# Attention scores in quarters of TensorE's array, and a softmax division moved from GpSimd to VectorE

## The chip, the cores and the metric

The kernel runs on one core of one Trainium2 chip. The metric is the device time of one execution in microseconds (us); lower is better. The core has five engines that work side by side: TensorE (PE in the profile, with its weight loads as PEld), VectorE (DVE), ScalarE (ACT), GpSimd (POOL) and SyncE (SP), which here issues nearly all transfers.

## The reference

The kernel computes a pooled attention and feeds its result to a gated two-layer network. There are 8 batches of 8 heads with 576 tokens and a head width of 64. Keys and values are averaged over groups of 8 tokens, so that 72 pooled positions are left per head.

```python
k_p = k.reshape(B, H, Sp, pool, D).mean(axis=3)        # Sp = 72, D = 64
v_p = v.reshape(B, H, Sp, pool, D).mean(axis=3)
scores = scale * np.matmul(q, k_p.transpose(0, 1, 3, 2))
scores = scores - np.max(scores, axis=-1, keepdims=True)
attn = np.exp(scores)
attn = attn / (np.sum(attn, axis=-1, keepdims=True) + 1e-09)
attn_out = np.matmul(attn, v_p)
x = attn_out.transpose(0, 2, 1, 3).reshape(B * S, H * D)   # 4608 x 512
h = x @ w_in                                               # 512 x 2048
out = (h * np.clip(h + 3.0, 0.0, 6.0) / 6.0) @ w_out       # 2048 x 512
```

All inputs and the output are fp32.

## The kernel before, in words

The 4608 tokens are cut into twelve blocks (`BLOCKS`: 512, 256, then ten of 384). The network is most of the work. The first four blocks run it directly (`Step.h` and `Step.out`, the matmuls of lines 841 and 872). The other eight are taken two at a time as "super blocks" that need seven products instead of eight: one stage of first-layer products (line 1127), then a stage of second-layer products (line 1204 or 1279). Operands are split into a high and a low part, so that one product is three matmuls on fp32r data, one record each in the trace. Scores are plain fp32, two records each.

The attention of a block is a list of small steps (`block_steps`). The steps of a later block are spread over the matmuls of an earlier one: the class `Paced` places a share of them at each slot between two products, so TensorE works on the network and on attention in turns. Instructions of attention on VectorE and ScalarE are kept behind the last instruction of the network that was marked on their engine (`mark`, `after_mark`), and the order of the first part of the program is written out by number in `ORDER` and set by `put_in_order`.

A block's tokens are cut into tiles of 128 (two halves of 64). Where a batch ends inside a tile, the tile has two parts of 64 tokens, one of each batch. For every tile:

- `load_q` loads the queries as [128 rows = two heads of 64, 4 pairs of heads, 128 tokens]. For a tile of two batches it makes two such tiles, each with the other half filled with zeros by GpSimd (line 241).
- `scores` is called twice, for 4 heads each (group g = 0, 1). `Scores.product` (line 465) makes for each of 2 pairs of heads one fp32 matmul with 128 rows, 128 tokens as weights and 144 columns streamed from `kbds`, a block-diagonal matrix with the pooled keys of two heads (72 each) and zeros elsewhere. A tile of two batches needs twice as many matmuls, which add up. `top` takes the negated maximum on VectorE (line 469), `exps` makes four exponentials with their sums on ScalarE (line 474), `invert` adds 1e-9 and takes the reciprocal on VectorE (lines 491 and 492), and `divide` multiplies on GpSimd from the third block on, in one product for 64 of the 72 positions of each head (line 503) and one for the other 8 (line 509).
- `transposes` (lines 574 and 576) turns the attention weights with TensorE, two steps to a tile, two or three groups behind the scores, and splits them with ScalarE and VectorE (lines 585 to 600).
- `av` multiplies with the pooled values (line 648), four steps for each part of a block that belongs to one batch, and ScalarE copies the result (line 650).

The outputs of these small matmuls use the PSUM banks named in `att_banks`, in turn: three (a0, a1, o3) in the first stage of a super block, two (a0, a1) in the second.

`plan` hangs the loading and preparing of K and V of a batch on earlier steps: K from `SIDE` = 12 steps before the first scores of that batch up to these scores (`load_k`, `prep_k`), V from the first scores up to the first product with the values (`load_v`, `prep_v`).

Of the kernel before, what the change touches and what calls it, by code (L numbers as in the profile page):

```python
# [8 lines left out]
F32 = mybir.dt.float32  # L9
# [19 lines left out]
SIDE = 12  # L29
# [36 lines left out]
        454-456 422-425 489-491 476-478 444-447 486-488 479-482 457-460 473-475 492-503 483-485 546-547  # L66
        513-515 504-506 540-542 572-573 554-556 507-509 557-559 543-545 548-550 592-593 551-553 510-512
        522-524 519-521 560-565 525-527 516-518 566-568 528-533 586-588 569-571 574-579 589-591 534-536
        594-599 580-582 537-539 583-585
# [4 lines left out]
        101 75 97 110 98 77-78 102 63 100 79 103 83 81 99 82 64 86 104 84 105 119 88 87 92 124 89 94 62 130  # L74
        93 106 95 125 108 107 120 111 115 109 117 121 116 118 131 128 112 126 134 127 129 68 136 132 66-67
        133 113 65 138 114 123 135 137 140 122 144 139 142 141 150 143 145 152 154 151 147 146 153 156
        148-149 155 157-158 160-161 169 165 163 166-168 170 176 171 164 159 172 181 173 162 182 174 183 175
        177 179-180 184 178 185
# [7 lines left out]
        175 183 177 180-181 179 187 186 184 188 185 194-197 189 202-205 198-199 182 200 208-211 190-191 201  # L86
        206 192 207 212-213 193
    """,
    "Pool": """
        0-1 12 2-3 18 4 7-8 10 5 9 6 14 13 16 15 17 11 19-20 24 21 23 22  # L90
# [3 lines left out]
        35 48 46 43 36 47 39 52 59 42 37-38 45 40 50 49 53-55 57-58 60 56  # L94
# [5 lines left out]
def attention_moe_kernel(  # L100
# [133 lines left out]
    def load_q(tile):  # L234

        qtiles[tile] = []
        for i, (b, s0, n, _) in enumerate(tile):
            t = pool.tile([P, NPAIR, P], F32, name="qt", bufs=2) if i == 0 else ring("qt")
            t = t if i == 0 else t[:, : NPAIR * P].rearrange("p (c t) -> p c t", c=NPAIR)
            if n < P:  # L240
                nc.gpsimd.memset(t[:, :, P // 2 :] if i == 0 else t[:, :, : P // 2], 0.0)
# [198 lines left out]

    class Scores:


        def __init__(self, tile, g):
# [7 lines left out]
            else:  # L452
                self.e = pool.tile([P, 4, SP], F32, name="e", bufs=2)
# [40 lines left out]
        def divide(self, engine):  # L494

            e, sm = self.e, self.sm
            if self.a is None:
# [15 lines left out]
                op=ALU.mult,  # L513
            )
            attn[self.tile, self.g] = self.a

    rests = {}

    def scores(j, tile, g):
# [1079 lines left out]
```

## Time and profile before

| what | value |
| --- | --- |
| time, median of 3 runs | 886.65 us (886.44 to 888.14) |
| the profiled execution: its own time | 887.28 us |
| the profiled execution: its span from first to last instruction | 885.5 us |
| granted TensorE clock, mean | 0.998 |
| ScalarE, exponentials of the attention (line 474, 256 of them) | 324 ns each |
| GpSimd, small division (line 509, 60 of them) | 389 ns each |
| transfers | 200.00 MB, mean 226 GB/s |

The profile comes from one execution. Durations of single instructions are its; a matmul's duration includes the pipeline behind its last element, so the distance of two starts says what it costs in a stream. Each fp32 matmul leaves two records, each with its own weight load. A time in front of a row is counted from the start of the span.

### The profile page before, as it was taken

To read this page: it belongs to the slowest core of one execution; us is meant where nothing else is said; L and a number is where in the kernel's file an instruction comes from. 1 tells how busy PE (TensorE), PEld (TensorE's weight loads), DVE (VectorE), ACT (ScalarE), POOL (GpSimd) and SP (SyncE) were. 2 spreads that over 40 slices of the span, in tenths; PEclk is the share of its full clock that TensorE was granted. 3 is DMA by queue.
4 is the path that set the end of the run, shared out by engine and by line. 5 is a ranking of instruction groups with operands and counts; after the bars stand their busy time and mean duration, and the time that the engine had idled before them with its cause. 6 is when DMAs were issued, how large, how long until landed. Compare 5 with 4: busy or idle time off the path is not lost.

```text
span 885.5 us, 15623 instructions
## 1 busy us (share of the span) xinstructions
PE 868.3 (98%) x5360; PEld 812.0 (92%) x5360; DVE 650.5 (73%) x1322; ACT 551.9 (62%) x1515; POOL 81.4 (9%) x168
## 2 busy tenths in 40 slices
PE   7999999999999999999999999999999999999998
PEld 7788888988989999999888999899999999999998
DVE  5887754567877885878888588987588887466664
ACT  6998766655666654887444688655576756354442
POOL 4100002110111100112000101100110200000000
PEclk9999999999999999999999999999999999999999
DMA  9970206995425254996697969877886687877784
GB/s 315 391 280 0 77 20 202 366 318 161 122 80 161 60 156 123 367 308 214 205 284 234 379 217 288 247 258 246 277 302 219 202 270 243 275 256 239 268 268 134
DMA packets 124654, 200.00 MB, mean 226 GB/s; under 512 B 13216, under 2 KB 81056, under 8 KB 124576
## 3 DMA queue, kind: packets, MB, share of 16 engines
q1 hardware_dynamic: 124432, 199.00, 68.7%
q8 instruction: 43, 0.70, 0.3%
q14 instruction: 35, 0.29, 0.1%
q10 hardware_dynamic: 144, 0.00, 0.0%
HBM read 158.08 MB, written 40.89 MB: 225 GB/s over the span
## 4 chain that ended last, share of the span: by engine, by line
PE 80%; DVE 7%; DMA 7%; ACT 3%; SPq 1%; issue 1%; DVEq 0%; ACTq 0%
PE psx L1127 21%; PE psx L1279 20%; PE pso L872 12%; PE psh L841 12%; PE psx L1204 7%; PE psa L648 4%; PE psa L465 3%; DMA wsFalse<-wd 2%; DMA stage<-q_l 2%; ACT e L474 2%; PE psa L574 1%; DMA wd<-wq 1%; DMA qt<-q_l 1%; DMA wsTrue<-wd 1%; DVE vst L385 1%
## 5 line engine op out<-in xcount | busy, mean ns | idle before, releaser
L1127 PE MATMUL psx<-x,wsFalse 128*128 128x384 f32 x768 | 150.8, 339 | 1.2 <-DMA wsFalse<-wd 1.2
L841 PE MATMUL psh<-xhi,w 128*128 128x384 f32 (+2 forms) x520 | 146.2, 340 | 0.1
L1127 PEld LDWEIGHTS psx<-x,wsFalse 128*128 128x128 f32 x768 | 132.7, 188 | 2.3 <-ACT part L1113 1.2
L1113 ACT CAST part<-g 128x768 fp32r<-128x768 f32 x100 | 83.3, 837 | 75.1 <-PE psx L1279 56.0
L872 PE MATMUL pso<-w,ghi 128*128 128x512 f32 x384 | 120.6, 399 | 0.4 <-ACT o L877 0.4
L1115 DVE TENSOR_TENSOR part<-g,part 128x768 fp32r<-128x768 f32 x100 | 95.1, 955 | 35.1 <-ACT part L1113 34.8
L1127 PE MATMUL psx<-x,wsTrue 128*128 128x384 f32 x576 | 116.1, 340 | 0.1
L1279 PE MATMUL psx<-wsFalse,part 128*128 128x256 f32 x864 | 109.6, 283 | 0.8 <-DVE g L1098 0.4
L1279 PEld LDWEIGHTS psx<-wsFalse,part 128*128 128x128 f32 x864 | 106.4, 190 | 1.6 <-ACT kept L1254 1.0
L1127 PEld LDWEIGHTS psx<-x,wsTrue 128*128 128x128 f32 x576 | 99.6, 188 | 0.8 <-DVE g L1092 0.4
L841 PEld LDWEIGHTS psh<-xhi,w 128*128 128x128 f32 x520 | 93.3, 188 | 7.5 <-DVE g L853 0.4
L474 ACT ACTIVATE e<-psa,mx 128x72 f32<-128x72 f32 x256 | 78.7, 324 | 31.4 <-DVE mx L469 29.7
L841 PE MATMUL psh<-xlo,w 128*128 128x384 f32 (+2 forms) x260 | 87.1, 336 | 0.0
L503 POOL TENSOR_TENSOR a<-e,sm 128x256 f32<-128x256 f32 x60 | 40.2, 671 | 504.4 <-DVE sm L492 414.8
L1279 PE MATMUL psx<-wsTrue,part 128*128 128x256 f32 x648 | 82.1, 283 | 0.0
L1279 PEld LDWEIGHTS psx<-wsTrue,part 128*128 128x128 f32 x648 | 79.6, 190 | 0.0
L1090 ACT ACTIVATE r<-g,small 128x384 f32<-128x384 f32 x96 | 58.5, 622 | 33.6 <-DVE g L1098 33.0
L872 PEld LDWEIGHTS pso<-w,ghi 128*128 128x128 f32 x384 | 68.9, 188 | 11.0 <-ACT o L877 0.7
L872 PE MATMUL pso<-w,glo 128*128 128x512 f32 x192 | 74.6, 399 | 0.0
L1098 DVE TENSOR_TENSOR g<-psx,c 128x384 f32<-128x384 f32 x96 | 52.0, 552 | 28.7 <-PE psx L1127 23.1
L1092 DVE SCALAR_TENSOR_TENSOR g<-r,g 128x384 f32<-128x384 f32 x96 | 54.6, 579 | 14.0 <-ACT r L1090 13.5
L1107 ACT COPY c<-psx 128x384 f32<-128x384 f32 x96 | 44.9, 485 | 23.8 <-PE psx L1127 23.7
(139 smaller groups left out, 1453.9 us busy)
## 6 DMA issues: line engine op xcount, KB each, us to landing
wsFalse<-wd SPq DMA_DIRECT2D x64, 512.0 KB, 4.8
wsTrue<-wd SPq DMA_DIRECT2D x48, 512.0 KB, 4.9
wsFalse<-w2d SPq DMA_DIRECT2D x31, 512.0 KB, 5.0
wsFalse<-w2t SPq DMA_DIRECT2D x27, 512.0 KB, 5.3
wsTrue<-w2d SPq DMA_DIRECT2D x21, 512.0 KB, 5.1
wsTrue<-w2t SPq DMA_DIRECT2D x21, 512.0 KB, 5.3
raw<-w_in_l SPq DMA_DIRECT2D x16, 512.0 KB, 8.4
raw<-w_out_l SPq DMA_DIRECT2D x16, 512.0 KB, 8.9
```

The costliest lines, as they stand in the source:

```text
L474: nc.scalar.activation(self.e[:, h], self.ps[:, h], AF.Exp, bias=self.mx[:, h : h + 1], accum_out=self.sm[:, h : h + 1])
L841: nc.tensor.matmul(self.ps, l[f][:, c, :], r[:, c, :], start=c == 0 and i == 0, stop=c == NCC - 1 and i == 2)
L872: nc.tensor.matmul(pos, l, r, start=f == 0 and i == 0, stop=f == NF - 1 and i == 2)
L1090: nc.scalar.activation(r, src, AF.Relu, bias=half_low, scale=GSCALE / (6.0 * WSCALE))
L1092: nc.vector.scalar_tensor_tensor(out=g_of[i][:, k], in0=r, scalar=GSCALE, in1=src, op0=ALU.min, op1=ALU.mult)
L1098: nc.vector.tensor_tensor(out=g_of[i][:, k], in0=ps, in1=kept, op=ALU.add)
L1107: nc.scalar.copy(c, ps)
L1113: nc.scalar.copy(t[:, 0], src)
L1115: nc.vector.tensor_tensor(out=t[:, 1], in0=src, in1=t[:, 0].bitcast(F32), op=ALU.subtract)
L1127: nc.tensor.matmul(ps, w[:, l, c * P : (c + 1) * P], t[:, r, c], start=o in (1, 2, 5) and c == 0 and k == 0, stop=c == 1 and k == 2, skip_ ...
L1204: nc.tensor.matmul(to, l, w[:, qs, r], start=f == 0 and k == 0, stop=end and k == 2)
L1279: nc.tensor.matmul(to, t[:, l, k, i * P : (i + 1) * P], w[:, k, r], start=begin and k == 0 and y == 0 and i % 2 == 0, stop=m == NM - 1 and ...
```

## The change

From the third block on (block index j > 1), `block_steps` uses the new class `TileScores` in place of two calls of `scores` per tile. It does this for all eight heads of a tile:

- `product` makes 16 fp32 matmuls: for each of 4 pairs, for each head r of the pair and for each half x of the tile's tokens, one with 64 rows (head r), 64 columns of weights (the half's queries) and 72 streamed elements (this head's pooled keys, without the zeros). Head r goes to bank r of two banks, half x to partitions 64x to 64x + 63. The four matmuls of a pair thus lie in four different quarters of the array. Outside the written-out part each is kept behind the one before it. The two maxima follow at once, one per bank (288 elements each).
- `exps(0)` and `exps(1)` make the exponentials of four heads each, as steps of their own.
- `finish`, in the same step as `exps(1)`, adds 1e-9 and takes the reciprocal once for eight heads, then makes four products, in place in the tile of the exponentials for the 64 positions. It runs on VectorE, but for the first tile of the third block, which stays on GpSimd.

The transposes of a tile follow a whole tile later; at the end of a block an empty step stands in front of them. `load_q` loads a tile of two batches into one tile without zero fills, and `Scores.product`, still used for the first two blocks, writes the two batches of a tile to their own partitions with 64 columns of weights each. `SIDE` becomes 16, V is prepared from two steps before the first scores on, and the numbers in `ORDER` follow the changed instructions.

```diff
-SIDE = 12
+SIDE = 16
...
+        t = pool.tile([P, NPAIR, P], F32, name="qt", bufs=2)
         for i, (b, s0, n, _) in enumerate(tile):
-            t = pool.tile([P, NPAIR, P], F32, name="qt", bufs=2) if i == 0 else ring("qt")
-            t = t if i == 0 else t[:, : NPAIR * P].rearrange("p (c t) -> p c t", c=NPAIR)
-            if n < P:
-                nc.gpsimd.memset(t[:, :, P // 2 :] if i == 0 else t[:, :, : P // 2], 0.0)
-            nc.sync.dma_start(t[:, :, i * (P // 2) : i * (P // 2) + n], q[b, :, :, s0 : s0 + n])
+            mine = t[:, :, i * (P // 2) : i * (P // 2) + n]
+            nc.sync.dma_start(mine, q[b, :, :, s0 : s0 + n])
             after_mark()
-            qtiles[tile].append(t)
+            qtiles[tile].append(mine)
...
-                for r, (qt, (b, _, _, _)) in enumerate(zip(qtiles[self.tile], self.tile)):
-                    nc.tensor.matmul(to, qt[:, p, :], kbds[b % 2][:, p, :], start=r == 0, stop=r == last)
+                for r, (qt, (b, _, n, _)) in enumerate(zip(qtiles[self.tile], self.tile)):
+                    nc.tensor.matmul(
+                        to[r * (P // 2) : r * (P // 2) + n], qt[:, p, :], kbds[b % 2][:, p, :], start=True, stop=True
+                    )
...
+    class TileScores:
...
+        def product(self):
+            tile = self.tile
+            banks = att_bank(), att_bank()
+            self.mx, self.sm = (pool.tile([P, NG, 4], F32, name=f"{m}s", bufs=2) for m in ("mx", "sm"))
+            halves = [slice(x * D, (x + 1) * D) for x in range(2)]
+            before = last_pe() if len(window) == 2 else None
+            for p in range(NPAIR):
+                for r in (1, 0):
+                    for x, half in enumerate(halves):
+                        part = x % len(tile)
+                        b = tile[part][0]
+                        nc.tensor.matmul(
+                            banks[r][half, p * SP : (p + 1) * SP],
+                            qtiles[tile][part][halves[r], p, half if len(tile) == 1 else slice(0, D)],
+                            kbds[b % 2][halves[r], p, r * SP : (r + 1) * SP],
+                            start=True,
+                            stop=True,
+                        )
+                        if before:
+                            behind(traced[-1], before)
+                        before = traced[-1].name
...
+            for r in (1, 0):
+                to = self.mx.rearrange("p g (i r) -> p (g i) r", r=2)[:, :, r]
+                nc.vector.tensor_reduce(out=to, in_=self.ps[r], axis=AX.X, op=ALU.max, negate=True)
+                self.later()
...
+        def finish(self, engine):
+            e, sm = self.e, self.sm
+            nc.vector.tensor_scalar(out=sm, in0=sm, scalar1=1e-9, scalar2=None, op0=ALU.add)
+            nc.vector.reciprocal(sm, sm)
+            rest = rests[self.tile] = pool.tile([P, NG, 2 * REM], F32, name="ar", bufs=2)
+            for g in range(NG):
+                to = e[:, g].rearrange("p h s -> p (h s)")[:, : 4 * D]
+                engine.tensor_tensor(
+                    out=rest[:, g].rearrange("p (c h s) -> p c h s", c=2, h=4),
+                    in0=e[:, g, None, :, D:].broadcast_to([P, 2, 4, SR]),
+                    in1=sm[:, g, None, :, None].broadcast_to([P, 2, 4, SR]),
+                    op=ALU.mult,
+                )
+                engine.tensor_tensor(
+                    out=to.rearrange("p (h s) -> p h s", h=4),
+                    in0=e[:, g, :, :D],
+                    in1=sm[:, g, :, None].broadcast_to([P, 4, D]),
+                    op=ALU.mult,
+                )
+                attn[self.tile, g] = to
...
-        for t in tiles_of[j]:
+        for n, t in enumerate(tiles_of[j] if j > 1 else ()):
+            x, by = TileScores(t), nc.vector if n or j > 2 else nc.gpsimd
+            steps.append((loads_behind(t), x.product, "scores", [b for b, *_ in t]))
+            steps.append(([], lambda x=x: x.exps(0), None, ()))
+            steps.append(([], lambda x=x, by=by: (x.exps(1), x.finish(by)), None, ()))
+            while todo:
+                turn()
+            todo.extend((t, g) for g in range(NG))
+        if j > 1:
+            steps.append(([], None, None, ()))
+
+        for t in tiles_of[j] if j < 2 else ():
...
-                side_steps(b), ("scores", "av"), (begin - SIDE, begin), (begin, uses("av", b)[0])
+                side_steps(b), ("scores", "av"), (begin - SIDE, begin), (begin - 2, uses("av", b)[0])
```

More of the change, by code (lines that the diff above doesn't have):

```diff
@@ L85 @@
         154 151 149 155 157 160 156 152 166 158 161 159 167 170-172 162-163 168 164 173 165 174 176 178 169
[L86 to L87 removed]
+        175 183 177 180-181 179 187 186 184 188 185 189 198-201 194-195 182 196 204-207 190-191 197 202 192
+        203 208-209 193
     """,
     "Pool": """
[L90 removed]
+        0-1 12 2-4 7-8 10 5 9 6 14 13 16 15 11 17-20
     """,
@@ L439, in pool_second @@
         place_rest(1, rest[:, :, :D])
+    exps_of = {}
     class Scores:
@@ L452, in __init__ @@
             else:
-                self.e = pool.tile([P, 4, SP], F32, name="e", bufs=2)
+                if g == 0:
+                    exps_of[tile] = pool.tile([P, NG, 4, SP], F32, name="e", bufs=2)
+                self.e = exps_of[tile][:, g]
                 self.a = None
@@ L459, in product @@
             ps = att_bank()
-            last = len(self.tile) - 1
             for i in range(2):
@@ L497, in divide @@
             if self.a is None:
-                self.a = pool.tile([P, 4 * D], F32, name="a", bufs=3)
                 if self.g == 0:
@@ L501, in divide @@
                 self.rest = rests[self.tile][:, self.g]
+                self.a = e.rearrange("p h s -> p (h s)")
             copies = 3 if self.first else 2
[L503 to L514 removed]
@@ L515, in divide @@
-            attn[self.tile, self.g] = self.a
+            main = self.a[:, : 4 * D].rearrange("p (h s) -> p h s", h=4), e[:, :, :D], sm[:, :, None].broadcast_to([P, 4, D])
+            rest = (
+                self.rest.rearrange("p (c h s) -> p c h s", c=copies, h=4),
+                e[:, None, :, D:].broadcast_to([P, copies, 4, SR]),
+                sm[:, None, :, None].broadcast_to([P, copies, 4, SR]),
+            )
+            for to, x, y in (main, rest) if self.first else (rest, main):
+                engine.tensor_tensor(out=to, in0=x, in1=y, op=ALU.mult)
@@ new lines, in divide, with last_pe, __init__, exps @@
+            attn[self.tile, self.g] = self.a
+    def last_pe():
+        return next(i for i in reversed(traced) if i.engine == mybir.EngineType.PE).name
+    class TileScores:
+        def __init__(self, tile):
+            self.tile = tile
+        def product(self):
[19 more added lines that the diff above has]
+                        before = traced[-1].name
+            self.ps = [x[:, : NPAIR * SP].rearrange("p (n s) -> p n s", s=SP) for x in banks]
+            self.e = pool.tile([P, NG, 4, SP], F32, name="e", bufs=2)
+            self.later = after_mark if late else no_slot
+            for r in (1, 0):
+                to = self.mx.rearrange("p g (i r) -> p (g i) r", r=2)[:, :, r]
+                nc.vector.tensor_reduce(out=to, in_=self.ps[r], axis=AX.X, op=ALU.max, negate=True)
+                self.later()
+        def exps(self, g):
+            for h in range(4):
+                nc.scalar.activation(
+                    self.e[:, g, h],
+                    self.ps[h % 2][:, 2 * g + h // 2],
+                    AF.Exp,
+                    bias=self.mx[:, g, h : h + 1],
+                    accum_out=self.sm[:, g, h : h + 1],
+                )
+                self.later()
+        def finish(self, engine):
[16 more added lines that the diff above has]
+                    op=ALU.mult,
+                )
+                attn[self.tile, g] = to
```

25 lines of the change are left out of this document (7 added, 18 removed).

## The prediction

> **What bounds the kernel now.** I read the page's busy lines first, then the chain that ended last, then the costliest groups kept apart by shape, and then TensorE's waits.
>
> ```profile
> PE 868.3 (98%) x5360; PEld 812.0 (92%) x5360; DVE 650.5 (73%) x1322; ACT 551.9 (62%) x1515; POOL 81.4 (9%) x168
> ...
> PE 80%; DVE 7%; DMA 7%; ACT 3%; SPq 1%; issue 1%; DVEq 0%; ACTq 0%
> ```
>
> TensorE is busy 98% of the span and holds 80% of the chain. What shortens its work shortens the kernel almost one for one; what lengthens VectorE, at 73%, costs nothing on average and can still cost in a crowded stage. So the first question is what the scores cost TensorE. First two places where they stand in the stream (start, duration, engine, line, operation, count), then their group and those of the softmax (count, busy time, mean ns of one, idle before):
>
> ```profile
> 38.50 1.14 PE L465 MATMUL psa<-kbd,qt 128*128 128x144 f32 x8
> ...
> 188.60 0.65 PE L465 MATMUL psa<-kbd,qt 128*128 128x144 f32 x4
> ```
>
> ```profile
> L465 PE MATMUL psa<-kbd,qt 128*128 128x144 f32 x288 | 45.8, 287 | 0.5 <-DVE arem L600 0.3
> ...
> L503 POOL TENSOR_TENSOR a<-e,sm 128x256 f32<-128x256 f32 x60 | 40.2, 671 | 504.4 <-DVE sm L492 414.8 <-ACT r L1090 24.2 <-ACT wq L945 17.3
> ...
> L469 DVE TENSOR_REDUCE mx<-psa 128x4 f32<-128x288 f32 x72 | 31.8, 450 | 15.5 <-PE psa L465 15.4
> ...
> L491 DVE TENSOR_SCALAR sm<-sm 128x4 f32<-128x4 f32 x72 | 14.0, 198 | 23.7 <-ACT e L474 19.6 <-POOL a L503 2.5 <-ACT stage L474 1.0
> ...
> L492 DVE RECIPROCAL sm<-sm 128x4 f32<-128x4 f32 x72 | 12.6, 176 | 1.7 <-DVE sm L491 0.2
> ...
> L241 POOL MEMSET qt<- 128x256 f32 x8 | 2.5, 315 | 39.8 <-DVE ksum L265 27.2 <-PE psa L465 11.2 <-DVE vlo L398 1.4
> ...
> L503 DVE TENSOR_TENSOR a<-e,sm 128x256 f32<-128x256 f32 x4 | 1.7, 420 | 0.0
> ...
> L509 DVE TENSOR_TENSOR ar<-e,sm 128x64 f32<-128x64 f32 x4 | 0.8, 216 | 0.0
> ```
>
> The 287 ns of one score record is mostly pipeline: four take 0.65 us, so they start (0.65 - 0.287) / 3 = 0.121 us apart, and eight take 1.14 us, which gives (1.14 - 0.287) / 7 = 0.122 us. That pitch, not 287 ns, is what a record costs TensorE. One fp32 matmul leaves two records here (a tile of one batch has 2 groups of 2 matmuls and the trace has 4 records in a group), so such a tile costs 8 x 0.122 = 0.98 us and a tile of two batches, with twice the matmuls, 1.95 us. From the third block on there are 30 tiles; batches change inside a tile at tokens 1728, 2880 and 4032, so 27 are of the first kind and 3 of the second: 26.4 + 5.9 = 32.2 us, 3.6% of the span. That is all that the change can work on in TensorE.
>
> **Part by part.** The sum is made against the profiled execution: span 885.5 us, its own time 887.3 us, which is 0.6 us above the median of 886.65 us.
>
> *Scores in quarters.* A tile now has 4 pairs x 2 heads x 2 halves of its tokens = 16 matmuls, each 64 rows by 64 columns of the array with 72 elements streamed, so 32 records. A record of 144 elements has a pitch of 0.122 us, one of 72 then 0.061 us if the stream sets it. The trace has no matmul in a quarter of the array, so I bound it. If four run at once, a tile costs 32 x 0.061 / 4 = 0.49 us; if two, 0.98 us; if none, 1.95 us. Against 32.2 us, 30 tiles then cost 14.6 (-17.6), 29.3 (-2.9) or 58.6 us (+26.3). One row speaks on the weight loads, which go from 8 to 32 a tile and from 128 columns to 64:
>
> ```profile
> 76.35 0.30 PEld L648 LDWEIGHTS psa<-a,vrem 96*128 96x128 f32 x2
> 76.41 0.39 PE L648 MATMUL psa<-a,vrem 96*128 96x64 f32 x2
> ```
>
> ```profile
> L648 PEld LDWEIGHTS psa<-a,vrem 96*128 96x128 f32 x8 | 1.2, 191 | 0.0
> ```
>
> Here fp32 matmuls stream only 64 elements (0.054 us by the pitch above), yet two weight loads of 128 columns take 0.30 us with 0.191 us for one, so they start 0.11 us apart: with a short stream the weight load sets the pitch. For 64 columns that is about 0.055 us, below the 0.061 us of the stream, so the loads alone don't push a quarter's pitch up. They do if all 32 go through one door (32 x 0.055 = 1.76 us). I take the middle between two and four at once, 0.046 us a matmul or 0.73 us a tile: consecutive matmuls name four different quarters and two banks, so there is always another quarter to start, but the two records of one matmul share a quarter and follow each other. 30 x 0.73 = 22.0 us, a gain of 10.2 us.
>
> *Changing the array's shape.* Each tile goes from the whole array to quarters and back, 60 changes that the trace never shows. The nearest row is a matmul that restarts an idle array:
>
> ```profile
> 197.19 0.44 PE L841 MATMUL psh<-xhi,w 128*128 128x384 f32 x1
> ```
>
> ```profile
> L841 PE MATMUL psh<-xhi,w 128*128 128x384 f32 x256 | 72.8, 341 | 0.1
> ```
>
> It takes 0.44 us instead of 0.341 us: 0.10 us for a first weight load of 128 columns with nothing to hide behind. For 64 columns that is 0.05 us, 3.0 us for 60 changes. The lower end is zero. The upper end is the whole tail of a record (0.287 - 0.122 = 0.165 us) with the 0.10 us load behind it, 0.27 us a change, 16 us. I stay near the lower end because only the first load of a run is exposed in the row. The Trainium skill, "TensorEngine Tiling (Array Packing)", Key Properties, speaks against the change here: it says that a change of tiling mode, unlike a change of tile, drains TensorE. By that the tail is paid at every change, and the sum would be some 10 to 13 us worse; no run here shows it yet.
>
> *The division on VectorE.* Per tile it gets two main products and two small ones, 2 x (420 + 216) = 1.27 us, on 29 tiles (the first tile of the third block stays on GpSimd): 36.9 us. It loses one add and one reciprocal per tile (198 + 176 ns), since both now serve eight heads: 30 x 0.374 = 11.2 us. Net +25.7 us on VectorE, to 676 us or 76%. The two maxima per tile stay (288 elements each). Behind these instructions on VectorE's queue stand the gate and split operations that TensorE needs next, so the cover is VectorE's slack, and it is thinnest here (columns: stretch, length, then busy time of PE, PEld, DVE, ACT, POOL, then clock, DMA share, GB/s):
>
> ```profile
> 380.00:420.00 40.00, 39.67 (x240) 38.56 (x239) 32.98 (x81) 29.88 (x107) 7.52 (x13) 1.00 0.80 248
> 500.00:540.00 40.00, 40.00 (x244) 39.79 (x243) 32.37 (x69) 29.89 (x92) 5.38 (x11) 1.00 0.80 266
> 540.00:580.00 40.00, 38.19 (x253) 37.51 (x252) 34.49 (x76) 29.01 (x91) 5.42 (x12) 0.96 0.85 272
> 660.00:700.00 40.00, 40.00 (x263) 39.87 (x261) 33.24 (x77) 29.61 (x98) 4.22 (x8) 1.00 0.68 213
> ```
>
> The 12 GpSimd instructions of the third stretch are about three tiles; three tiles' net of 0.90 us bring VectorE from 34.5 to 37.2 of 40 us. That still fits.
>
> *GpSimd's wait goes.* TensorE's waits (us in total, times, longest) name the division on GpSimd, and one place and the stretch behind it show what it did:
>
> ```profile
> PE psa L574 <- POOL a L503: 2.1, 2, 1.4
> ...
> PE psa L648 <- DVE a L565: 0.9, 2, 0.5
> ```
>
> ```profile
> 565.99 0.44 PE L574 MATMUL psa<-ident,a 128*128 128x128 f32 x2 [1.38 <-POOL a L503]
> ```
>
> ```profile
> 567.20:570.80 3.60, 3.60 (x18) 3.60 (x19) 3.48 (x9) 3.02 (x7) 0.00 (x0) 0.53 0.93 307
> ```
>
> The transpose of the weights of attention waited 1.38 us, and right behind it the granted clock was 0.53 for 3.6 us, worth another 1.7 us: 3.8 us with the other wait. A later transpose (a tile behind instead of two groups behind) takes the place of these waits, but the reciprocal and the V loads ahead of it can be late too, so I count half, -2 us.
>
> *Longer bursts.* A tile's chain grows: two maxima instead of one, eight exponentials in a row, one late division for all heads, and two banks held from the first product to the last exponential. In the last stage of a super block there are only two banks for all of attention. The chain shows what four exponentials take (8 records with their sums):
>
> ```profile
> 191.63 1.22 ACT e L474 x8
> ```
>
> If whatever follows in the two banks waits for the second four, that is 1.2 us; at most once in each of ten blocks, 12 us; zero if the pacing spreads it. I count +2 us, since the steps of a tile lie apart in time by more than that. Only the last tile of a block has little time to its transposes (two steps); the others have a whole tile's steps.
>
> *Edits with one answer.* Eight zero fills of q tiles on GpSimd go (0.315 us each, on an engine that is 9% busy). The same q loads are issued, into one tile instead of two. Loading and preparing K up to 16 steps ahead instead of 12, and V from two steps earlier, follow the greater number of steps in a block, so in time they move little; SP's queue keeps its number of transfers. The hand-written order of the start moves a few instructions. The one two-batch tile of the second block now uses 64-column matmuls too: 16 records, at most 0.98 us gained, left out of the sum.
>
> Sum: -10.2 + 3.0 - 2 + 2 = -7.2 us, 880.1 us in the profiled execution's terms, **879.5 us** against the median.
>
> **Rivals.**
>
> *Four at once.* All quarters run together; a tile costs 0.49 us, 7.3 us below the forecast: 872 us. For it: four neighbours in the stream never share a quarter. Against: both records of a matmul do.
>
> *Two at once.* Starts stay in the order of issue, so a matmul's second record waits 0.061 us for its first, and the next quarter waits behind it: 16 x 0.061 = 0.98 us, what a tile costs today. Gain 2.9 instead of 10.2 us: 887 us, no difference. The Trainium skill, "TensorE: Matmul & The Clock Gate", Part 3, The mechanism, has a rule that leads here: packed matmuls start and end strictly in program order, though neighbours in different tiles may start some nanoseconds apart. No run here shows it yet, since the trace of before has no packed matmul.
>
> *VectorE becomes the bound.* Where it is already over 80% busy (380-420, 500-580 and 660-700 us; their 44 GpSimd instructions are some 11 tiles) the 0.90 us that each tile adds delays the gate or the split of the next product and TensorE waits as long: 11 x 0.90 = 10 us, 890 us, slower. It decides once TensorE's idle time in these stretches grows by over 7 us. For it: 34.5 of 40 us. Against: the largest wait of TensorE on VectorE in the list above is 0.9 us in all.
>
> *No overlap.* The quarters run one after another, so the change doesn't do what it says: +26.3 instead of -10.2 us, 916 us, slower. For it: the 0.11 us pitch of weight loads shows that they can set the pace. Against: nothing but the quarters' independence.
>
> **How the numbers follow.** Forecast 0.48, four at once 0.16, two at once 0.12, VectorE 0.12, no overlap 0.12. Measurements of this kernel can tell 0.2%, 1.8 us, from no change. The first two are faster and hold 0.64; of "two at once" most is within 0.2% and the rest goes each way; of VectorE's case a little falls back within or below it: faster 0.66, same 0.10, slower 0.24. The range goes from 868 us (four at once with GpSimd's waits fully gone) to 893 us (VectorE's case with its drains); outside it stay "no overlap" and a few hundredths at the ends. The forecast's own range is 875 to 884 us.
>
> **What would show it.** Right: 32 score records a tile within about 0.75 us from first to last start, TensorE's score work down by 10 us, the next record after each run late by about 0.05 us, VectorE near 676 us, no TensorE wait on GpSimd. Wrong: a score run of 1 us or more, a restart of 0.2 us at each change of shape, TensorE waits on VectorE or on exponentials (banks) of several us in the stretches above, or a low clock somewhere new.

## The result and the profile after

The changed kernel takes 896.0 us (median of 4 runs, 894.66 to 896.6) against 886.55 us before (886.44 to 888.14): a ratio of 1.0101 with a 95% interval of 1.0085 to 1.0117, so 9.5 us or 1% slower (the 886.65 us given above was the median of the three runs there were then). The profiled execution spans 894.5 us. The page has these two lines (busy time of each engine, and the chain that ended last):

```profile
PE 867.8 (97%) x6056; PEld 798.2 (89%) x6056; DVE 658.1 (74%) x1378; ACT 550.6 (62%) x1515; POOL 19.7 (2%) x44
...
PE 71%; DVE 12%; DMA 8%; ACT 4%; SPq 2%; issue 2%; DVEq 0%; ACTq 0%
```

TensorE's share of the chain falls from 80 to 71%, and VectorE's rises from 7 to 12%. VectorE's busy time rises by only 7.6 us. The scores themselves do what they should. Three rows of the timeline, around one tile, and the group of all of them:

```profile
192.23 0.34 PE L919 MATMUL psh<-xhi,w 128*128 128x384 f32 x1
192.50 0.73 PE L534 MATMUL psa<-kbd,qt 64*64 64x72 f32 x32
193.16 0.44 PE L919 MATMUL psh<-xhi,w 128*128 128x384 f32 x1
193.43 0.34 PE L919 MATMUL psh<-xlo,w 128*128 128x384 f32 x1
```

```profile
L534 PE MATMUL psa<-kbd,qt 64*64 64x72 f32 x960 | 22.8, 230 | 0.8 <-ACT e L554 0.8
```

A record takes 230 ns, and 32 of them end 0.73 us after the first began: their starts span 0.50 us, 16 ns apart on average, where 0.061 us would be one after the other. The single records of the trace show how: they start in fours, 6 to 7 ns apart within a four and 62 to 63 ns from one four to the next (113 ns to the second). All four quarters run at once, each at the 0.061 us that the prediction gave to one record. The first record starts 0.27 us after a network matmul instead of the usual 0.17 (0.10 us late); behind the last start pass 0.16 us to the next record, and that one costs another 0.10 us. The tile as a whole costs 1.20 - 2 x 0.173 = 0.85 us instead of 0.98; over all 30 tiles I read 0.86 us, so TensorE's score work is 32.2 - 25.8 = 6.4 us shorter.

The loss lies elsewhere. I set the start of every network matmul of the two traces against its namesake: the difference is +1.3 us at 348 us, +9.0 at 358 us and +8.6 at the end. (It goes up and down by a few us in between, since scores now stand at other places.) That is the start of the first super block. The longest of TensorE's waits after, then VectorE's and TensorE's timeline there, and stretches with their granted clock (length, busy time of PE, PEld, DVE, ACT, POOL, then clock, DMA share, GB/s):

```profile
PE psx L1205 <- DVE g L1176: 4.1, 1, 4.1
```

```profile
353.24 0.69 DVE L1024 TENSOR_TENSOR wq<-wq 128x512 fp32r<-128x512 f32 x1 [0.73 <-ACT wq L1023]
358.50 0.56 DVE L1176 TENSOR_TENSOR g<-psx,c 128x384 f32<-128x384 f32 x1 [4.56 <-DMA wd<-wq]
```

```profile
349.43 0.40 PE L950 MATMUL pso<-w,glo 128*128 128x512 f32 x1
...
353.64 1.34 PE L1205 MATMUL psx<-x,wsFalse 128*128 128x384 f32 x6 [0.53 <-ACT c L1185]
359.11 3.25 PE L1205 MATMUL psx<-x,wsFalse 128*128 128x384 f32 x9 [4.13 <-DVE g L1176]
```

```profile
355.00:356.00 1.00, 0.00 (x0) 0.00 (x0) 0.00 (x0) 0.56 (x2) 0.00 (x0) 1.00 0.92 336
356.00:359.00 3.00, 0.00 (x0) 0.00 (x0) 0.50 (x1) 0.00 (x0) 0.00 (x0) 0.51 0.98 269
359.00:363.00 4.00, 3.89 (x12) 3.75 (x13) 2.59 (x10) 2.80 (x11) 0.00 (x0) 0.51 0.98 352
```

What are `wq` and `wd`? The super blocks multiply with sums of first-layer weights. VectorE and ScalarE make them beside the third and fourth block, in 16 links (`sums_of`). Each link fills the tile `wq`; four transfers store it to DRAM (`wd`), from where the super blocks load it as `ws`. There is one `wq`, so a link's first instruction waits for the stores of the link before. The first gate product `g` of the super block lies in memory that `wq` had. So after the last link ended at 353.9 us (353.24 + 0.69), its stores had to land, the gate product began at 358.5, and TensorE stood 4.1 us. Its granted clock was half for 6.8 us, from 356.1 to 362.9 us. TensorE stood idle for the first 3.0 us of that, so the slow clock met 3.8 us of work and cost 1.9 us. (The expectations below count the whole 6.8 us, 3.4 us lost; that is too much.) In the kernel before, the last link ended at 347.6 us, 0.5 us ahead of the last matmul of the plain blocks at 348.1:

```profile
346.93 0.69 DVE L946 TENSOR_TENSOR wq<-wq 128x512 fp32r<-128x512 f32 x1 [0.73 <-ACT wq L945]
...
348.11 0.40 PE L872 MATMUL pso<-w,glo 128*128 128x512 f32 x1
```

Of the 7.7 us between the two places (+1.3 and +9.0), 4.7 are waits (4.13 and 0.53), 1.9 the clock; most of the rest is that two whole tiles of scores stand in this stretch, where the kernel before has half a tile.

Why was it late? VectorE's waits between 300 and 350 us, first before, then after:

```profile
DVE g L853 <- ACT g L849: 5.4, 6, 1.8
...
DVE wq L939 <- DMA wd<-wq: 0.6, 1, 0.6
```

```profile
DVE wq L1017 <- DMA wd<-wq: 7.7, 4, 3.6
...
DVE g L931 <- ACT g L927: 1.4, 3, 0.7
```

Before, VectorE had other work while the stores of a link were under way, and in this stretch lost 0.6 us to them. After, the link's first instruction (line 1017) comes to the head of VectorE's queue too early and holds up everything behind it for 7.7 us in all. (Over all 16 links it is 12.5 us before and 19.6 after.) The links have run out of room: the last ones follow each other at the pace of compute, store and wait.

TensorE's second-longest wait is new too (0.1 us before). It is for the gate of the plain blocks:

```profile
PE psh L919 <- DVE g L931: 3.4, 5, 1.0
```

The longest of these five, at 267 us, stands behind a link that had itself waited 4.1 us for stores; what made the other four is not shown.

### The profile page after: what moved, and what is told of

Its sections match the earlier page's. It is cut to its first block, busy times and chain, and to the rows that moved or that the text cites. A ratio compares the mean times of both kernels' runs of the same rounds, so it can differ in the third digit from the quotient of the medians.

```text
span 894.5 us, 16699 instructions
## 1 busy us (share of the span) xinstructions
PE 867.8 (97%) x6056; PEld 798.2 (89%) x6056; DVE 658.1 (74%) x1378; ACT 550.6 (62%) x1515; POOL 19.7 (2%) x44
## 4 chain that ended last, share of the span: by engine, by line
PE 71%; DVE 12%; DMA 8%; ACT 4%; SPq 2%; issue 2%; DVEq 0%; ACTq 0%
PE psx L1205 22%; PE psx L1357 19%; PE psh L919 9%; PE pso L950 8%; PE psx L1282 7%; PE psa L715 3%; DMA wd<-wq 3%; ACT e L554 1%; PE psa L534 1%; SPq L1026 1%; DMA raw<-w_in_l 1%; PE psa L641 1%; DVE g L1170 1%; DMA wsFalse<-wd 1%; DMA raw<-w_out_l 1%
## 5 line engine op out<-in xcount | busy, mean ns | idle before, releaser
L1205 PE MATMUL psx<-x,wsTrue 128*128 128x384 f32 x576 | 113.8, 339 | 0.1
L919 PEld LDWEIGHTS psh<-xhi,w 128*128 128x128 f32 x520 | 93.1, 188 | 12.7 <-DVE g L931 4.7
L950 PEld LDWEIGHTS pso<-w,ghi 128*128 128x128 f32 x384 | 69.0, 188 | 12.5 <-ACT o L955 0.8
L554 ACT ACTIVATE e<-psa,mxs 128x72 f32<-128x72 f32 x240 | 73.2, 329 | 11.1 <-DVE mxs L549 10.9
L1176 DVE TENSOR_TENSOR g<-psx,c 128x384 f32<-128x384 f32 x96 | 52.2, 551 | 28.8 <-PE psx L1205 17.9
L950 PE MATMUL pso<-w,glo 128*128 128x512 f32 x192 | 72.8, 396 | 0.0
L1170 DVE SCALAR_TENSOR_TENSOR g<-r,g 128x384 f32<-128x384 f32 x96 | 52.2, 552 | 13.7 <-ACT r L1168 13.4
L935 ACT CAST ghi<-g 128x384 fp32r<-128x384 f32 (+2 forms) x65 | 33.1, 509 | 32.5 <-DVE g L931 30.9
```

Of the source, the lines that this page charges most:

```text
L554: nc.scalar.activation(self.e[:, g, h], self.ps[h % 2][:, 2 * g + h // 2], AF.Exp, bias=self.mx[:, g, h : h + 1], accum_out=self.sm[:, g, ...
L919: nc.tensor.matmul(self.ps, l[f][:, c, :], r[:, c, :], start=c == 0 and i == 0, stop=c == NCC - 1 and i == 2)
L950: nc.tensor.matmul(pos, l, r, start=f == 0 and i == 0, stop=f == NF - 1 and i == 2)
L1170: nc.vector.scalar_tensor_tensor(out=g_of[i][:, k], in0=r, scalar=GSCALE, in1=src, op0=ALU.min, op1=ALU.mult)
L1176: nc.vector.tensor_tensor(out=g_of[i][:, k], in0=ps, in1=kept, op=ALU.add)
L1205: nc.tensor.matmul(ps, w[:, l, c * P : (c + 1) * P], t[:, r, c], start=o in (1, 2, 5) and c == 0 and k == 0, stop=c == 1 and k == 2, skip_ ...
```

## The experiments

Each run has a ratio to runs of the kernel before on the same chip (medians 886.3 to 887.8 us in the five groups).

### First group: is it the late chain or VectorE's load?

Theory A: one chain is late at one place. Theory B: VectorE's greater load. Differences to the changed kernel are taken from its 896.0 us, which come from another set of runs; taken from the ratios they differ by up to 1.6 us.

`e1_share45`, attention of the sixth block asked for earlier:

```diff
-        (3, att_steps(5), (), 0.6),
+        (3, att_steps(5), (), 0.45),
```

> The changed kernel with one number edited: the attention of the sixth block is spread over 0.45 instead of 0.6 of the slots of the fourth block, so it ends earlier. Theory A (one late chain): the changed kernel loses its time in one place, where the first super block starts. The sixth block's attention ends later, the operands made from it come later on VectorE, the last weight sums behind them end at 354 instead of 348 us, and the first gate product waits for them (4.1 us) and pays a halved clock after that (about 3.4 us). Then this kernel takes some 7 us less than the changed one, about 889 us, its last weight sum ends before 349 us and the 4 us wait is gone. Theory B (VectorE's load): the divisions on VectorE delay gates and splits all over the kernel; then this stays within 2 us of 896 us.

Measured 896.76 us, ratio 1.010 (1.0079 to 1.0122). The edit missed its aim: the scores stayed at the same places in TensorE's order (all runs of score records but two, which moved by a few matmuls), which behind the numbered part is made when the program is built, from modelled times. The last link ended at 354.6 us. It tells nothing between A and B.

`e2_pool_div`, all divisions on GpSimd as before:

```diff
-            x, by = TileScores(t), nc.vector if n or j > 2 else nc.gpsimd
+            x, by = TileScores(t), nc.gpsimd
```

> The changed kernel with all divisions of the new class on GpSimd, as before the change. Theory B (VectorE's load): the 36 us of divisions are the loss, so this takes 888 us or less. Theory A (one late chain): the late chain stays, 894 to 898 us, with the wait of about 4 us at the start of the first super block still there.

Measured 893.18 us, 1.0051 (1.0034 to 1.0067): 2.8 us better. That is just below what A said (894 to 898) and far above what B said (888 or less); the wait at the first super block is still there (3.5 us in two). But the last link now ended at 347.8 us, as early as before, and 6.3 us were still lost at that place. So the link's clock time alone isn't it; more on this below.

`e3_before_vec_div`, the kernel before with the divisions on VectorE:

```diff
-        s.divide(nc.vector if j == 1 else nc.gpsimd)
+        s.divide(nc.vector if j == 1 or len(window) == 2 else nc.gpsimd)
```

> The kernel before with only the engine of the division changed: VectorE instead of GpSimd, from the first tile behind the written-out part on. Theory B (VectorE's load): slower by 5 to 10 us, 892 to 897 us. Theory A (one late chain): within 2 us of 886.6 us, since the steps and their places stay as they were.

Measured 890.75 us, 1.0028 (1.0015 to 1.0041). Between the theories: the division alone costs some 3 us. The table below puts 2.4 us of them at the same place.

`e4_full`, the changed kernel with scores by the whole array, four heads to a bank, for 29 of the 30 tiles:

```diff
+                        nc.tensor.matmul(
+                            banks[p // 2][part * D : part * D + n, p % 2 * 2 * SP : (p % 2 + 1) * 2 * SP],
+                            qtiles[tile][part][:, p, :],
+                            kbds[b % 2][:, p, :],
```

> The changed kernel with the scores made by the whole array again (four matmuls of 144 elements a tile, eight for a tile of two batches, one bank for four heads); grouping by tile, division, pacing stay as changed. The rows of the two traces say that a tile of one batch costs TensorE 0.98 us on the whole array and 0.86 us in quarters with the change of shape included, so theory A and theory B both expect 3 to 7 us more than the changed kernel, 899 to 903 us; if the quarters were no gain, 896 us or less.

Measured 888.85 us, 1.0013 (0.9996 to 1.003). Both theories missed (899 to 903). Taking the quarters away gains 7 us, though they make TensorE's work shorter. The last link ended at 346.7 us and no long wait followed there.

### Second group: the quarters, or the order that is made of them?

I wrote one kernel's order of instructions on every engine, behind the written-out part, into the other (a list of numbers, set with `behind` as `put_in_order` does).

```python
for x, y in zip(numbers, numbers[1:]):
    behind(by[mine[y]], end.get(mine[x], mine[x]))
```

`e6_full_in_quarter_order`, whole-array scores in the changed kernel's order:

> The mirror image: whole-array scores, in the order of the changed kernel. Theory C: 896 plus 6 us of score work = 902, 898 to 905, and the wait on the gate product near 350 us is back. Theory D: 887 to 890, without that wait.

Measured 898.28 us, 1.0129 (1.0105 to 1.0153). The long wait is back, and of the 30 tiles only the first still uses quarters:

```profile
PE psx L1410 <- DVE g L1381: 4.1, 1, 4.1
```

So the wait comes with the order, not with what the quarters do on the chip. With the same work as `e4_full` it is 9 us slower. Against the changed kernel, which has the same order, it also gives the price of the quarters themselves: they are 2.3 us faster than the whole array, though TensorE's score work is 6.4 us less.

`e5_quarters_in_full_order`, the mirror image:

> The changed kernel, with the instructions of TensorE, VectorE, ScalarE, GpSimd and the DMA queue from the third block on put into the order that the kernel with whole-array scores (888.85 us) has; a tile's 32 records stand where the last of its whole-array matmuls stood. Theory C (the quarters cost nothing on the chip beyond their own 0.86 us a tile; what was lost comes from the order that the scheduler makes of them): 888.9 less some 6 us of score work = 883, 880 to 886, with no wait of several us on the gate product near 350 us. Theory D (the quarters themselves cost the rest of the engines or the clock something, in any order): 892 to 898.

Measured 903.71 us, 1.0185 (1.0163 to 1.0206). A clear miss. TensorE now waited for exponentials:

```profile
PE psa L831 <- ACT e L742: 13.3, 8, 3.1
```

The records stood where the second half of the whole-array matmuls had been, so the first half's exponentials came too late for the transposes. `e16_quarters_at_first` (run later) put them where the first half had been:

> Quarters in the order of the kernel with whole-array scores, as in the run of that name, but with a tile's records and maxima where the first of its whole-array matmuls and maxima stood, so that the exponentials start no later than there. Order is the loss: 888.9 - 6 = 883, 880 to 886, and the waits on exponentials are gone. The quarters cost something on the chip in any order: 892 to 898.

Measured 904.26 us, 1.0188 (1.0164 to 1.0212), and another wait had taken the place:

```profile
PE psa L718 <- ACT e L742: 8.1, 5, 3.3
```

L718 is the score product itself. Eight heads at once need two free banks at once, and one of them is still being read by the exponentials of the tile before; two groups of four need one bank at a time. So the order of one doesn't fit the other at either end, and these two runs don't give the price of the quarters. Both lie above either forecast (880 to 886, or 892 to 898).

`e7_side12`, the plan of K and V loads as before:

```diff
-SIDE = 16
+SIDE = 12
...
-                side_steps(b), ("scores", "av"), (begin - SIDE, begin), (begin - 2, uses("av", b)[0])
+                side_steps(b), ("scores", "av"), (begin - SIDE, begin), (begin, uses("av", b)[0])
```

> The changed kernel with the side steps of a block planned as before (12 steps ahead instead of 16, the second half 2 steps later). If the plan's shift makes the late chain: 887 to 890. If the place that the scheduler gives the quarters does: 894 to 898.

Measured 890.67 us, 1.0026 (1.0009 to 1.0044): 5.3 us of the 9.5 go with the two numbers of the plan. The last link ended at 349.7 us, and no halved clock followed.

`e8_quarter_after_quarter`, a tile's products sorted by quarter:

```diff
-            for p in range(NPAIR):
-                for r in (1, 0):
-                    for x, half in enumerate(halves):
+            for r in (1, 0):
+                for x, half in enumerate(halves):
+                    for p in range(NPAIR):
```

> The kernel of the first of these runs with a tile's 16 products sorted by quarter, so that eight records in a row use the same quarter, where neighbours used different ones. If quarters run beside each other only when neighbours differ: a whole-array record of 144 columns takes 0.122 us, so one of 72 some 0.061; 32 of them 1.96 us instead of 0.51 us, 29 tiles: 42 us above the first run. If order inside a tile does not matter: within 2 us of the first run.

Measured 919.09 us, 1.0363 (1.0335 to 1.039), 15.4 us above `e5_quarters_in_full_order` ("the first run"), between the two forecasts. The run of a tile:

```profile
194.20 1.63 PE L718 MATMUL psa<-kbd,qt 64*64 64x72 f32 x32
```

Starts are (1.63 - 0.23) / 31 = 0.045 us apart on average instead of 0.016: most follow at 56 to 63 ns, and only some start with a neighbour, 5 to 6 ns behind it. So neighbours in different quarters are what makes them overlap. 29 tiles x 0.9 us are 26 us; some 4 us of that took the place of waits for exponentials (13.3 us in `e5`, 9.0 here), and where the rest went I didn't settle.

### Third group: move the wait

`e9_gate_elsewhere`: the gate tiles of the first super block are allotted in reverse order, so that the first doesn't lie on `wq`. TensorE's order is unchanged.

```diff
+        if n == 0:
+            for i in reversed(range(0, NPR, 2)):
+                pairs[i // 2] = late[1].tile([P, 2, 4, HALF], F32, name=f"g{i}")
```

> The changed kernel with one edit: the gate's result tiles of the first super block are allotted in the reverse order, so that the first gate product writes memory that the weight sums' tile wq did not lie in. TensorE's order stays what it was. If the loss is the late weight-sum chain that the first gate product waits for: the 4.1 us wait and the halved clock of 6.8 us behind it (3.4 us) go, 896 - 7.5 = 888.5, 887 to 890. If something else on the way is late as well and takes the wait's place: 893 to 896.

Measured 895.94 us, 1.009 (1.0076 to 1.0104): nothing gained. The gate's wait is gone and this one has come:

```profile
PE psx L1208 <- DMA wsTrue<-wd: 4.7, 1, 4.7
```

The super block also loads the sums that the last link stores. The second reader of the chain was late by as much as the first. With the same edit, `e10_gate_pool` (divisions on GpSimd), `e11_gate_side12` (plan as before) and `e12_gate_side12_pool` (both):

> The same edit on the changed kernel with all divisions on GpSimd (893.18 us with its wait of 3.5 us and 3.4 us for the halved clock). Late chain: 893.2 - 6.9 = 886.3, 885 to 889. VectorE's load as a second term of its own: 2 to 4 us below the run with the divisions on VectorE and the tiles elsewhere; if the divisions only acted through the late chain: within 1 us of it.

> The same edit on the changed kernel with the plan of the side steps as before (890.67 us, waits on the gate product of 2.5 us in all and no halved clock). Late chain: 890.7 - 2 = 888.7, 888 to 890.5. If the plan costs by itself, beside the chain: 2 us or more below the run with the new plan and the tiles elsewhere.

> Quarters alone: plan as before, divisions on GpSimd as before, and the gate's tiles elsewhere. The score work of TensorE is 6.5 us less than before. If nothing else is lost: 887.4 - 6.5 = 881, 880 to 884. If the divisions cost nothing and a loss of 8 us that is neither chain nor division remains: within 1.5 us of the run with the plan as before, near 889.

Measured 895.05 us (1.0075, 1.0058 to 1.0091), 891.16 us (1.0038, 1.0024 to 1.0052) and 892.19 us (1.0046, 1.0032 to 1.0059). In each the wait for `ws` stands in the gate's place (4.0, 2.2 and 2.5 us), so the gains that a vanished chain was to bring (885 to 889, 888 to 890.5 and 880 to 884 us) did not come; for the third neither forecast held. The plan is worth 4.8 us here with the divisions on VectorE and 2.9 with them on GpSimd; the divisions 0.9 us, or nothing.

### Fourth group: shorten the chain itself

`e13_one_sum_less` and, as control, `e14_before_one_sum_less` leave out one of the 16 sums and store the sum before it a second time in its place, so their output is not the reference's:

```diff
+        if (i, h) == (NPR - 1, 0):
+            t = last_sums[0]
+            for o, at in {7: 0, 3: 1, 5: 2, 6: 3}.items():
+                nc.sync.dma_start(dram_of(i, o)[:, :, half], t[:, :, at])
+            return
```

> The changed kernel without the work of one of the 16 weight sums, the last but one: its stores are made from the sum before it, so that the transfers stay and one link of the chain (some 8 us) is gone; the output is not the reference's. If the late end of the weight sums is the loss: the wait at the first super block goes, 896 - 7.5 = 888.5, 887 to 890. If it is only a place where time shows that was lost earlier: 893 to 896.

> Control: the kernel before with the same link left out. Its last weight sum ends before the plain blocks do, so nothing should wait for it: 887.4 within 1.5. If the 4 us of VectorE work that is left out pays by itself: 883 to 885.

Measured 889.08 us (1.002, 1.0007 to 1.0034), 7 us better than the changed kernel, and 885.84 us (0.998, 0.9964 to 0.9997), 1.8 us better than before, between the control's two forecasts. So up to 1.8 of the 7 us may come from the work left out, and at least 5 from the chain. In the first, the last link ends ahead of its block, and VectorE's gate product waits for its operand alone:

```profile
348.18 0.69 DVE L1032 TENSOR_TENSOR wq<-wq 128x512 fp32r<-128x512 f32 x1 [0.69 <-ACT wq L1031]
...
353.97 0.56 DVE L1184 TENSOR_TENSOR g<-psx,c 128x384 f32<-128x384 f32 x1 [1.69 <-PE psx L1213]
```

`e15_two_sums_tiles` keeps all sums but breaks the chain: high parts and sums get tiles of their own, two for the sums, each link makes eight stores instead of four, and the links of the fourth block are asked for earlier. To make room, the ring of small tiles has 3 instead of 4 (`e17` and `e18` below too).

```diff
-        return pool.tile([P, S], F32, name=name, tag="ring", bufs=4)
+        return pool.tile([P, S], F32, name=name, tag="ring", bufs=3)
...
-        t = early_x[-1].tile([P, 2, 4, P], F32, name="wq", bufs=1)
-        hi, q = t[:, 0], t[:, 1]
+        hi = early_x[-1].tile([P, 4, P], F32, name="wh", bufs=1)
+        q = early_x[-1].tile([P, 4, P], F32, name="wq", bufs=2)
...
-        hooks[2 + n // NPR].setdefault(2 * (n % NPR), []).append(step)
+        hooks[2 + n // NPR].setdefault(2 * (n % NPR) if n < NPR else 3 * (n - NPR) // 2, []).append(step)
```

> The changed kernel with all weight sums, but with a tile of their own for the high parts and two for the sums, so that a sum need not wait for the stores of the one before, and asked for earlier in the last plain block; the ring of small tiles has 3 instead of 4 to make room. If the late end of the weight sums is the loss: 887 to 891. If not, or if the doubled number of stores or the shorter ring cost as much: 893 to 898.

Measured 889.18 us, 1.002 (1.0006 to 1.0035), 6.8 us better, with no sum left out. TensorE's order is another one here too, so the run by itself doesn't tell the two tiles from the earlier links. The last link ends 17 us ahead:

```profile
327.44 0.69 DVE L1024 TENSOR_TENSOR wq<-wq,wh 128x512 fp32r<-128x512 f32 x1 [2.46 <-ACT wh L1023]
```

For every kernel, how late the last link ends against the start of the last matmul of the plain blocks, and how long from there to the 61st first-layer record of the super block, both read from the traces in us:

| kernel | late | then |
| --- | --- | --- |
| before | -0.5 | 10.2 |
| before, one sum less | -5.7 | 9.9 |
| quarters, two sums tiles (`e15`) | -17.0 | 10.4 |
| the same, plan as before (`e18`) | -15.8 | 10.8 |
| the same, plan and divisions as before (`e17`) | -12.8 | 10.8 |
| quarters, one sum less | -1.5 | 10.7 |
| whole array (`e4_full`) | 0.1 | 10.9 |
| before, division on VectorE | 1.6 | 12.7 |
| quarters, plan as before | 2.0 | 13.6 |
| quarters, division on GpSimd | 2.2 | 16.5 |
| quarters in the whole array's order (`e16`, `e8`, `e5`) | 1.0, 1.4, 1.6 | 14.4, 13.3, 12.8 |
| gate elsewhere, plan or divisions or both as before (`e12`, `e11`, `e10`) | 1.5, 1.7, 2.0 | 14.0, 15.2, 16.4 |
| attention of the sixth block earlier (`e1`) | 4.0 | 19.2 |
| **the changed kernel** | 4.5 | 17.9 |
| quarters, gate elsewhere | 4.5 | 18.1 |
| whole array in that order | 4.6 | 18.2 |

Where the link ends no later than 0.1 us, the stretch takes 9.9 to 10.9 us; at 1.0 to 2.2 us late 12.7 to 16.5; at 4 us and more 17.9 to 19.2. This also settles the second run: there the plain blocks ended 3.8 us earlier than in the changed kernel and the link 6.1 us earlier, which left it 2.2 us late. It matters which comes last, and not when.

### Fifth group: what is left

`e17_two_sums_side12_pool` (two sums tiles, plan and divisions as before, so of the change only the quarters and the grouping by tile) and `e18_two_sums_side12` (the same with the divisions on VectorE):

> Quarters with the weight sums in two tiles, the plan of the side steps as before and the divisions on GpSimd as before. If the plan and the divisions take the gain away: 882 to 886, below both kernels. If TensorE's saved 6.5 us is lost to waits for other engines whichever they are: 887 to 891.

> The same with the divisions on VectorE. If the divisions cost by themselves: 2 to 4 us above the run with GpSimd's; if only the plan matters: the same as it and below the run with the new plan (889.2), near 885; if neither: 888 to 891.

Measured 883.7 us (0.9963, 0.9951 to 0.9975) and 885.18 us (0.9983, 0.9972 to 0.9994). The first beats both kernels: 2.6 us below before and 12 below the changed kernel. Its busy line and chain:

```profile
PE 863.4 (98%) x6056; PEld 797.0 (90%) x6056; DVE 639.9 (73%) x1262; ACT 549.7 (62%) x1515; POOL 80.6 (9%) x160
...
PE 77%; DVE 8%; ACT 5%; DMA 5%; SPq 3%; issue 1%; DVEq 0%; ACTq 0%
```

With the late chain out of the way, the plan costs 889.2 - 885.2 = 4.0 us and the divisions 1.5 us. The two profiled executions put most of the plan's 4.0 us at another single place: at 427 us, in the first super block, `e15` waits for a copy on ScalarE and runs at half the granted clock from 428.9 to 432.3 us, and `e18` does neither.

```profile
PE psa L715 <- ACT x L717: 1.9, 1, 1.9
```

Two tiles for the sums weren't run on the kernel before; one sum less was worth 0.2% there, so about half of the 0.37% may belong to the chain and not to the quarters.

## Why the prediction was wrong

The forecast was 879.5 us and faster; the kernel is 1% slower, outside the range of 868 to 893 us.

*Scores in quarters* (-10.2) and *changing the array's shape* (+3.0): the net of -7.2 us stood against -6.4 us measured, but both terms were mis-sized, and that their sum came out near is luck. A tile's records span 0.50 us and not 0.73, as in the rival "four at once". Going in and coming out cost 0.10 and 0.26 us, 0.36 us a tile, where I had 0.10. Not all of it is the change of shape: behind four whole-array score records of the kernel before, too, the next record costs 0.10 us more, but it starts 0.03 us behind the last start instead of 0.16. The rule in the Trainium skill, "TensorEngine Tiling (Array Packing)", Key Properties, that a change of mode drains TensorE points the way of these rows, but they don't show a whole drain: 0.16 us is less than the 0.23 us that the last record takes. The rival "two at once" falls: four records start within 20 ns, so the second record of a matmul didn't hold up the next quarter by 0.061 us. On this, "TensorE: Matmul & The Clock Gate", Part 3, The mechanism, in the Trainium skill (starts some nanoseconds apart) agrees with the trace, 6 to 7 ns; what I drew from its strict order did not.

*The division on VectorE* (net +25.7 us, hidden): VectorE grew by 7.6 us only. Its new groups are near the forecast (417 and 220 ns for one division where I had 420 and 216, but 32.6 us busy in all where I had 36.9, since neighbours overlap; and 11.1 us less for adds and reciprocals), but some of its other work became shorter where GpSimd no longer ran beside it. The gate's second step, in the changed kernel and in the one with the divisions on GpSimd:

```profile
L1170 DVE SCALAR_TENSOR_TENSOR g<-r,g 128x384 f32<-128x384 f32 x96 | 52.2, 552 | 13.7 <-ACT r L1168 13.4
```

```profile
L1170 DVE SCALAR_TENSOR_TENSOR g<-r,g 128x384 f32<-128x384 f32 x96 | 54.6, 576 | 14.6 <-ACT r L1168 14.3
```

Even so it wasn't hidden: 1.5 to 3.4 us in three pairs of runs, 0.9 us or nothing in two. The stretches that I checked for cover lay between 380 and 700 us; the one that mattered, ahead of 350 us, I did not look at.

*Edits with one answer.* This is one of the two steps that failed: "Loading and preparing K up to 16 steps ahead instead of 12, and V from two steps earlier, ... so in time they move little". Those two numbers cost 2.9 to 5.3 us in four pairs of runs, a good part of the whole loss, and the working had them at nothing. I named no work that hides them and didn't ask what else VectorE has to finish before the super block.

*GpSimd's wait goes* (-2): it went; no TensorE wait after is on GpSimd's division, and the slow clock behind it went too. One wait of 0.9 us on VectorE's division (line 576) is new. *Longer bursts* (+2) named two banks held at once as the risk. TensorE waited only 0.8 us for banks in the order that was made; in an order made for another kernel (`e16`) it was 8.1 us.

*What shortens TensorE's work shortens the kernel almost one for one.* This was the assumption behind the sum, the other step that failed and the larger one: it broke at 348 us. There a second chain, the weight sums, ended 0.5 us ahead of TensorE. What TensorE saved before that could bring at most half a microsecond, and any delay of the chain had to show at once, and more than in full: the chain ended 4.5 us late, and the stretch took 7.6 us longer (17.9 instead of 10.2), with 4.1 us of waiting for the stores and 1.9 us for the halved clock in it. Elsewhere it didn't hold in full either: in the same order the 6.4 us less of score work were worth 2.3 us. The 7% of DMA and 7% of VectorE in the chain of before were on the page, and I didn't follow them to their place.

*VectorE becomes the bound* was the rival nearest to the truth, with 890 us and the right sign, but neither its place nor its mechanism held: VectorE wasn't too busy, it stood still behind an instruction that waited for a store.

Still open is which of the reordered steps makes the links late, and where the rest of the 6.4 us goes. That the order does it is shown by the pair `e4_full` and `e6_full_in_quarter_order`; that the links collide with the combining of the first super block's inputs (line 1116), which VectorE also does between 320 and 336 us, is only argued.

## What to carry to other kernels

Where a stage ends in a hand-over (tiles stored, read back, or freed for the next stage), look up how far apart the chains that meet there end. The one that ends half a microsecond earlier is as much the bound as the one on top. An edit of "when" (a plan, a lead, a share) is not free because it adds no instruction: in a program whose order is made from modelled times it moves every engine's queue, and a wait at the head of an in-order queue holds up all that stands behind it. When a wait is removed by moving memory, ask who else reads the same data.

## What the runs showed of the hardware

- Quarters of the array overlap fully: 32 fp32 records of 64 rows, 64 columns and 72 elements start 16 ns apart on average when neighbours use different quarters (in fours, 62 to 63 ns from four to four), and 45 ns apart on average when eight in a row use the same one.
- Going to quarters and back cost 0.10 + 0.26 us a tile, of which 0.10 us also stands behind whole-array score records.
- The granted clock was half for 6.8 us around a 4.1 us gap in TensorE's work, from 1.1 us after the gap began (356.1 us), and for 3.4 us around one of 4.7 us (`e9`), from 0.3 us ahead of its end. The kernel before had such a stretch too, 3.4 us at 567 us, 1.3 us behind its wait of 1.4 us; a wait of 1.3 us in the changed kernel at 570 us had none.
- Some of VectorE's operations were slower when GpSimd made its divisions beside them: the gate's second step 576 to 579 instead of 552 ns, the split of the gate's low part (`glo`) 591 to 592 instead of 553 ns in three kernels, but 558 in `e17`, also with GpSimd's divisions. The gate's first product, which reads PSUM, was not (552 and 551 ns).
